# Attention and mixture of experts on one core: score chains of four heads, PV in single tiles, and what reads PSUM in the general path

## The chip, the cores and the metric

One core of one Trainium2 chip runs the whole program. The metric is the device time of one execution in microseconds (us); the median of several executions is given. Engines are PE (TensorE matmuls, PEld its weight loads), DVE (VectorE), ACT (ScalarE), POOL (GpSimd) and SP (SyncE, which issues most DMAs).

## The reference

```python
scores = scale * np.matmul(q, k.transpose(0, 1, 3, 2))      # B=4, H=8, S=768, D=64
keep = is_sink | in_window                                   # 4 sinks, window 128
scores = np.where(keep, scores, -1000000000.0)
a = np.exp(scores - np.max(scores, axis=-1, keepdims=True))
a = a / (np.sum(a, axis=-1, keepdims=True) + 1e-09)
x = np.matmul(a, v)                                          # -> (3072, 512)
logits = x @ w_gate + modality_bias[modality_id]             # 8 experts
e_idx = np.argmax(logits, axis=1)
for e in range(E):
    h = np.maximum(x[mask] @ w1[e], 0.0)                     # mask = e_idx == e, F = 1024
    out[mask] = gate_w[mask, None] * (h @ w2[e])
h = out @ w_in                                               # 512 -> 2048
return (h * (1.0 / (1.0 + np.exp(-1.702 * h)))) @ w_out
```

## The kernel before

The program has four stages in one launch. `attention` (L41) works on 24 tiles `t` of 128 tokens, six for each of four batches, `i = t % 6`; a tile has 8 heads in 4 pairs `c`, two heads `a` beside one another on the array, and a half-tile `g` is two pairs. A query tile sees its own 128 keys, the 128 before and the four sinks, so a score row has 260 columns, and 128 at `i = 0`. In the order of one tile:

- `qtrans`/`ktrans` (L156, L167) transpose queries and keys on PE into PSUM, `qevac` on ACT and `kevac` on DVE copy them out.
- `scores(t, c)` (L194) multiplies for two heads; `mask` (L202, DVE) adds the mask and takes the row maximum, `expo` (L211, ACT) writes the exponentials and their sums.
- `ptrans(t, c)` (L224, L225) transposes the probabilities of two heads; `pevac` copies them to `pts`, DVE for odd `c` (L242), ACT for even (L244). `pts` is a ring of three tiles.
- `pv` (L282) multiplies the values of a key tile with the probabilities of the two query tiles that see it, 256 columns in one product; at `i = 5` the last key tile has 128 columns more (L284). It accumulates in two PSUM banks `ops` that `zero` (L268, ACT) has filled with zeros.
- `oevac` (L291, ACT) copies a half-tile of the output, `back` transposes it back (L301, with a product for the sinks at L298) into PSUM, DVE divides by the sums (L319). Then follow `norm`, `logits` and `pick`, the choice of the expert.

The order of the work is written as a table: `AT` gives for each kind a time in steps of a quarter-tile after the tile's own start, `OPEN` and `MORE` those of the next stage's first work, and `kinds` says how many quarters a call covers. All calls are sorted by time and emitted; each engine runs its instructions in that order. PSUM has eight banks: `NS_BUFS` = 3 for scores, `NT_BUFS` = 3 that `qtrans`, `ktrans`, `ptrans` and `back` share under one tag `t`, and 2 for `ops`. `fill` (L344) issues products without use to PE, 20 before the first scores.

Ahead of it, L1071 and L1072 load a flag into a register on each engine and branch: `general` (L515) is a slow path for other window sizes. It is skipped here, but its buffers share addresses with those of `attention`. After the branch DVE builds the masks (L494 to L507).

Routing sorts tokens by expert. `pair(u, units)` (L1407) runs an expert's 256 tokens; 8 pairs always run, up to 15 by a count known at run time, 12 here, each under an `If`. `more_alone` (L1522) then runs experts on 128 further tokens, 2 here; inside it `second_alone` (L1486) has an `If` (L1496) for the loads of the next expert's weights. `hint` (L1288) tells an engine's branch ahead of time which way it will go, from a register that `values_load` fills (L1290). Last, a dense stage of six groups of 512 tokens (`up`, L1170, and `down`, L1177) multiplies each operand in high and low parts.

Of the kernel before, what the change touches and what calls it, by code (L numbers as in the profile page):

```python
# [29 lines left out]
AT = dict(sinkevac=13.229, oevac=13.14, qevac=-3.201, kevac=-0.864, scores=-0.497, mask0=0.153, mask1=0.329, expo0=0.53, ptrans=2.608, pevac=3.3,  # L30
          expo1=1.235, pv=6.555, qtrans=-4.329, ktrans=-1.83, back=14.129, sinktrans=12.315, norm=14.975, logits=18.7, then=19.826, pick=23.746,
          guard=7.159, invert=12.135, zero=5.2, sinksplit=8.053)
PVU = 2
# [3 lines left out]
OPEN = dict(split1=2.989, x0=5.244, split0=4.299, x1=5.358, split2=5.494, split3=6.448, first0=6.769, first1=7.711, split4=14.718)  # L37
MORE = 85.058, 0.617, 92.724, 1.445


def attention(tc, cst, late, first, spare, q, k, v, wg, xd, then, pick, at_tile, more, opening):  # L41
# [8 lines left out]
    with ExitStack() as ctx:  # L50
# [33 lines left out]
        NV, NG = 6, 3  # L84
        zs = per.tile([P, 1], F32, name="zs")
        nc.gpsimd.memset(zs, 0.0)


        pts = per.tile([P, NG, 4, 2, 2, P], F32, name="pts")
        ops = [ps_o.tile([P, 2, 2, P], F32, name=f"ops{i}") for i in range(2)]  # L90
# [79 lines left out]
        def kevac(t):  # L170
            nc.vector.tensor_copy(kts[:, :, t % NT, 0:P], tps[("k", t)])
# [10 lines left out]
        def scores(t, c):  # L182
# [30 lines left out]
        def where(t, kk):  # L213

            return kk if t % NG else 1 - kk

        def ptrans(t, c):
            i = t % NT
            ps = ps_t.tile([P, 2, 2, P], F32, name=f"pt{t}_{c}", tag="t")
            k0, k1 = where(t, 0), where(t, 1)  # L220
            for a in range(2):
                h = 2 * c + a
                if i > 0:
                    nc.tensor.transpose(ps[:, k0, a, :], pn[t][:, h, 0:P], ident)  # L224
                    nc.tensor.transpose(ps[:, k1, a, :], pn[t][:, h, KB : KB + P], ident)  # L225
                else:
                    nc.tensor.transpose(ps[:, k1, a, :], pn[t][:, h, 0:P], ident)
            tps[("p", t, c)] = ps

        def pview(t, c, x):  # L230
            if t % NT == 0:
                return x[:, t % NG, c, :, t % 2, :]
            a, b = sorted(((t - 1) % NG, t % NG))
            return x[:, a : b + 1 : b - a, c, :, t % 2, :]

        def psrc(t, c):
            ps = tps[("p", t, c)]
            return ps[:, where(t, 1)] if t % NT == 0 else ps

        def pevac(t, c):  # L240
            if c % 2:
                nc.vector.tensor_copy(pview(t, c, pts), psrc(t, c))  # L242
            else:
                nc.scalar.activation(out=pview(t, c, pts), in_=psrc(t, c), func=AF.Copy)  # L244
# [25 lines left out]
        def pv(t, g=None):  # L270

            i = t % NT
            if i == 0:
                return
            kw = dict(start=False, stop=False, skip_group_check=True)
            for j in [t - 1] + ([t] if i == NT - 1 else []):
                for h in range(H) if g is None else range(4 * g, 4 * g + 4):

                    c, a = divmod(h, 2)
                    o = ops[c // 2][64 * a : 64 * a + 64, c % 2]  # L280
                    if j == t - 1:
                        nc.tensor.matmul(o.rearrange("p i t -> p (i t)"), nat[j]["v"][:, h], pts[:, j % NG, c, a].rearrange("p i t -> p (i t)"), **kw)  # L282
                    else:
                        nc.tensor.matmul(o[:, t % 2, :], nat[j]["v"][:, h], pts[:, j % NG, c, a, t % 2, :], **kw)  # L284
# [3 lines left out]
        def oevac(t, g):  # L288
            if g == 0:
                ohl[t] = late.tile([P, 4, P], F32, name=f"oh{t}", tag="oh", bufs=1)  # L290
            nc.scalar.activation(out=ohl[t][:, 2 * g : 2 * g + 2], in_=ops[g][:, :, t % 2, :], func=AF.Copy)  # L291
# [50 lines left out]
        def fill(n):  # L342
            for _ in range(n):
                nc.tensor.matmul(ops[1].rearrange("p c i t -> p (c i t)")[:, 0:256], cst["nothing"][:, 0:P], cst["nothing"], start=True, stop=True)  # L344
# [3 lines left out]
        def ok(t):  # L348
# [3 lines left out]
        kinds = dict(sinkevac=(4, sinkevac), oevac=(2, oevac), qevac=(4, qevac), kevac=(4, kevac), scores=(1, scores), mask0=(1, lambda t, c: mask(t, 2 * c)),  # L352
                     mask1=(1, lambda t, c: mask(t, 2 * c + 1)), expo0=(1, lambda t, c: expo(t, 2 * c)), expo1=(1, lambda t, c: expo(t, 2 * c + 1)),
                     ptrans=(1, ptrans), pevac=(1, pevac), pv=(PVU, pv), qtrans=(4, qtrans), ktrans=(4, ktrans), back=(2, back), sinktrans=(4, sinktrans), norm=(2, norm), logits=(4, logits), then=(4, lambda t: then(t, lgs.pop(t))), pick=(4, pick), guard=(4, guard), invert=(4, invert), zero=(2, zero), sinksplit=(4, sinksplit))
# [3 lines left out]
        for g in range(2):  # L358
            todo.append((len(F2) + .001, zero, (0, g)))
# [1285 lines left out]
```

## Time and profile before

| | |
|---|---|
| median of 3 runs | 1104.44 us (1102.95 to 1104.8) |
| the profiled execution: its own time | 1102.95 us |
| its span in the trace | 1101.4 us |
| mean granted clock of PE | 0.989 |
| busy: PE, DVE, ACT, POOL | 1068.0, 553.7, 418.2, 241.9 us |

Instructions carry the line of kernel.py that issued them. For an engine, a wait is listed with its releaser, the event that ended it; "issue" is time for which nothing is shown. Weight loads (PEld) are issued just ahead of the matmul they belong to, so their start times show the order and the pace of PE. An f32 matmul of the source appears as two instructions.

### The profile page before, as it was taken

To read this page: it belongs to the slowest core of one execution; us is meant where nothing else is said; L and a number is where in the kernel's file an instruction comes from. 1 tells how busy PE (TensorE), PEld (TensorE's weight loads), DVE (VectorE), ACT (ScalarE), POOL (GpSimd) and SP (SyncE) were. 2 spreads that over 40 slices of the span, in tenths; PEclk is the share of its full clock that TensorE was granted. 3 is DMA by queue.
4 is the path that set the end of the run, shared out by engine and by line. 5 is a ranking of instruction groups with operands and counts; after the bars stand their busy time and mean duration, and the time that the engine had idled before them with its cause. 6 is when DMAs were issued, how large, how long until landed. Compare 5 with 4: busy or idle time off the path is not lost. (4 is left out here: it accounts for less than half of the span.)

```text
span 1101.4 us, 18806 instructions
## 1 busy us (share of the span) xinstructions
PE 1068.0 (97%) x6625; PEld 904.5 (82%) x6625; DVE 553.7 (50%) x1385; ACT 418.2 (38%) x1026; POOL 241.9 (22%) x397
## 2 busy tenths in 40 slices
PE   6999999978999999999989999999999999999996
PEld 4676767668999999999978888888888888888885
DVE  3767767886555665522114665655623424334232
ACT  3887778742223332222222332332323222222221
POOL 2532231253243342211001213222200101001011
PEclk8999999998999999999999999999999999999998
DMA  6555565451445532216561322302203303124011
GB/s 122 127 125 126 112 138 118 103 146 60 136 123 161 181 98 79 79 52 197 172 217 55 115 83 73 113 8 70 77 1 115 91 24 116 32 83 153 1 39 39
DMA packets 172115, 108.91 MB, mean 99 GB/s; under 512 B 118000, under 2 KB 149744, under 8 KB 171984
## 3 DMA queue, kind: packets, MB, share of 16 engines
q1 hardware_dynamic: 167184, 91.62, 30.1%
q0 software_dynamic: 4800, 15.73, 4.3%
q8 instruction: 60, 0.98, 0.4%
q14 instruction: 71, 0.58, 0.2%
HBM read 79.85 MB, written 27.48 MB: 97 GB/s over the span
## 5 line engine op out<-in xcount | busy, mean ns | idle before, releaser
L1170 PE MATMUL pu<-xh,wah 128*128 128x256 f32 (+1 forms) x576 | 185.6, 322 | 0.0
L1170 PE MATMUL pu<-xh,wal 128*128 128x256 f32 (+1 forms) x576 | 184.2, 320 | 0.4 <-DVEq L1279 0.4
L1555 DVE TENSOR_TENSOR raw<-pu,raw 128x512 f32<-128x512 f32 x96 | 66.3, 691 | 235.2 <-ACT raw L1554 232.7
L1170 PE MATMUL pu<-xl,wah 128*128 128x256 f32 (+1 forms) x576 | 184.2, 320 | 0.1
L1554 ACT ACTIVATE raw<-pu 128x512 f32<-128x512 f32 x96 | 57.5, 598 | 291.9 <-PE pu L1170 291.2
L1185 PE MATMUL pa<-h,wah 128*128 128x256 f32 x768 | 155.4, 286 | 0.0
L1185 PEld LDWEIGHTS pa<-h,wah 128*128 128x128 f32 x768 | 128.0, 194 | 0.0
L1170 PEld LDWEIGHTS pu<-xh,wal 128*128 128x128 f32 x576 | 110.4, 192 | 8.2 <-DVEq L1279 0.6
L1170 PEld LDWEIGHTS pu<-xh,wah 128*128 128x128 f32 x576 | 110.5, 192 | 7.8 <-ACTq L1279 0.2
L1170 PEld LDWEIGHTS pu<-xl,wah 128*128 128x128 f32 x576 | 110.3, 192 | 7.8 <-DVE xl L1123 0.3
L1185 PE MATMUL pa<-h,wal 128*128 128x256 f32 x384 | 109.6, 285 | 0.0
L1193 ACT ACTIVATE h<-pu 128x256 fp32r<-128x256 f32 x96 | 36.8, 383 | 184.2 <-PE pu L1170 182.6
L202 DVE CUSTOM_DVE_ANT_0 sc<-s,m 128x260 f32<-128x260 f32 (+1 forms) x192 | 73.0, 399 | 51.9 <-PE s L194 46.9
L1196 DVE SCALAR_TENSOR_TENSOR h<-pu,h 128x256 fp32r<-128x256 f32 x96 | 40.3, 422 | 110.8 <-ACT h L1193 61.7
L211 ACT ACTIVATE pn<-sc,mx 128x260 f32<-128x260 f32 (+1 forms) x192 | 92.0, 482 | 5.4 <-DVE mx L202 4.7
L1122 ACT ACTIVATE h<-raw 128x512 fp32r<-128x512 f32 x96 | 60.7, 633 | 77.7 <-DVE raw L1555 77.7
L1177 PE MATMUL pa<-wah,h 128*128 128x512 f32 x216 | 76.4, 390 | 0.0
L1177 PE MATMUL pa<-wbh,h 128*128 128x512 f32 x216 | 76.3, 389 | 0.0
L1170 PE MATMUL pu<-xh,wbh 128*128 128x512 f32 x192 | 74.8, 390 | 1.2 <-ACT y L1493 1.2
L1170 PE MATMUL pu<-xh,wbl 128*128 128x512 f32 x192 | 74.7, 389 | 0.0
L1170 PE MATMUL pu<-xl,wbh 128*128 128x512 f32 x192 | 74.7, 389 | 0.0
L1185 PEld LDWEIGHTS pa<-h,wal 128*128 128x128 f32 x384 | 74.6, 194 | 0.0
(327 smaller groups left out, 2055.8 us busy)
## 6 DMA issues: line engine op xcount, KB each, us to landing
raw<-in_moe_w_dram SPq DMA_DIRECT2D x64, 256.0 KB
cd<-yb SPq DMA_DIRECT2D x20, 512.0 KB
xd<-xe SPq DMA_DIRECT2D x24, 256.0 KB
raw<-yp SPq DMA_DIRECT2D x12, 512.0 KB
qn<-in_q_dram SPq DMA_DIRECT2D x22, 256.0 KB
kn<-in_k_dram SPq DMA_DIRECT2D x22, 256.0 KB
vn<-in_v_dram SPq DMA_DIRECT2D x22, 256.0 KB
yb<-y SPq DMA_DIRECT2D x10, 512.0 KB
```

The source lines that it names most:

```text
L202: nc.vector.tensor_tensor_reduce(out=sc[:, :n], in0=ps[:, :n], in1=m[:, :n], scale=1.0, scalar=3.0e38, op0=ALU.add, op1=ALU.min, accum_out=mx)
L211: nc.scalar.activation(out=pn[t][:, h, :n], in_=sc[:, :n], func=AF.Exp, scale=-1.0, bias=mx, accum_out=sums[t][:, h : h + 1])
L1122: A.activation(out=hi, in_=x, func=AF.Copy)
L1170: nc.tensor.matmul(ps[:, 0:n], w[a][:, s], cols(x, b, k), start=(k == 0 and i == 0), stop=(k == 3 and i == 2))
L1177: nc.tensor.matmul(acc, h[a][:, s], w[b][:, 512:], start=(f == 0 and j == 0), stop=(f == last and j == 2))
L1185: nc.tensor.matmul(acc[:, i % 2 * 256 : i % 2 * 256 + 256], wa[f][a][:, s], h[b], start=(f == 0 and i % 2 == 0 and j == 0), stop=(f == CH ...
L1193: A.activation(out=hi, in_=ps, func=AF.Relu)
L1196: V.scalar_tensor_tensor(out=lo, in0=ps, scalar=0.0, in1=hi.bitcast(F32), op0=ALU.max, op1=ALU.subtract)
L1554: A.activation(out=s, in_=ps, func=AF.Sigmoid, scale=1.702)
L1555: V.tensor_tensor(out=s, in0=ps, in1=s, op=ALU.mult)
```

## The change

- `scores` takes a half-tile: four heads in one call, with a bank each (`NS_BUFS` 4); `AT`, `OPEN` and `MORE` have new times, those behind `pv` about three steps sooner.
- `pv` works on one query tile at a time, 128 columns a product, own keys and the keys before, with start and stop flags, in one bank `ops`. `zero` and the ring are gone; `pts` is a tile of a pool with two buffers.
- `kevac` of the first tile is on ACT.
- In `general`, ACT alone copies from PSUM, and its pools are on the right side of the memory.
- `hint` is a static hint within an `If` on a count that is already in a register; two rows of `sx` are gone; the counts are loaded at f = 3 instead of 5; the hints stand at f = 5, 3 and 2 instead of 6.
- The `If` in `second_alone` is on a register of SP alone.

```diff
-        def scores(t, c):
+        def scores(t, g):
...
-            for a in range(2):
+            for c, a in ((2 * g, 0), (2 * g, 1), (2 * g + 1, 0), (2 * g + 1, 1)):
...
         def kevac(t):
-            nc.vector.tensor_copy(kts[:, :, t % NT, 0:P], tps[("k", t)])
+            if t == 0:
+                nc.scalar.activation(out=kts[:, :, 0, 0:P], in_=tps[("k", t)], func=AF.Copy)
+            else:
+                nc.vector.tensor_copy(kts[:, :, t % NT, 0:P], tps[("k", t)])
...
-        def zero(t, g):
-            nc.scalar.activation(out=ops[g][:, :, t % 2, :], in_=zs.unsqueeze(2).broadcast_to([P, 2, P]), func=AF.Copy)
...
-            for j in [t - 1] + ([t] if i == NT - 1 else []):
-                for h in range(H) if g is None else range(4 * g, 4 * g + 4):
...
-                    if j == t - 1:
-                        nc.tensor.matmul(o.rearrange("p i t -> p (i t)"), nat[j]["v"][:, h], pts[:, j % NG, c, a].rearrange("p i t -> p (i t)"), **kw)
...
+            for c in (2 * g, 2 * g + 1):
+                for kk in range(i == 0, 2):
+                    for a in range(2):
+                        nc.tensor.matmul(ops[64 * a : 64 * a + 64, c], nat[t - 1 + kk]["v"][:, 2 * c + a], pts[t][:, c, kk, a], start=(kk == 0 or i == 0), stop=(kk == 1), skip_group_check=True)
...
-NS_BUFS = 3
+NS_BUFS = 4
...
-        per = ctx.enter_context(tc.tile_pool(name="ge1", bufs=1))
+        per = ctx.enter_context(tc.tile_pool(name="ge1", bufs=1, side="right"))
...
-                    V.tensor_copy(pr[:, j], pt)
+                    nc.scalar.activation(out=pr[:, j], in_=pt, func=AF.Copy)
...
-    def hint(label, row, i):
-        v = nc.values_load(sx[0:1, row, i : i + 1], engines=ENGINES, min_val=0, max_val=1)
-        tc.mark_branch_hint_location(label, v, engines=ENGINES)
+    def hint(label, n, i):
+        with tc.If(n <= i):
+            tc.mark_branch_hint_location(label, "LikelyTaken", engines=ENGINES)
...
-            if f == 5 and u == NP0 - 1:
+            if f == 3 and u == NP0 - 1:
                 counts()
-            if f == 6 and NP0 - 1 <= u < NP - 1:
-                hint(f"pairs{u + 1}", 7, u + 1)
+            if f == (5 if u == NP0 - 1 else 3) and NP0 - 1 <= u < NP - 1:
+                hint(f"pairs{u + 1}", pairs[0], u + 1)
...
+        alone.append(flag(2, E + 1, (ET.SP,)))
...
-            with tc.If(alone[0] > s + 1):
+            with tc.If(alone[1] > s + 1):
```

On PE, a half-tile in the middle of attention before (tile 9's scores, tile 8's transposed probabilities, tile 6's values):

```order
L194 MATMUL s9_0_0_2313<-kts_1141,qt9_2195 128x260
L194 MATMUL s9_0_1_2315<-kts_1141,qt9_2195 128x260
L224 MATMUL pt8_1_2318<-ident_97,pn8_2223 128x128
L225 MATMUL pt8_1_2318<-ident_97,pn8_2223 128x128
L224 MATMUL pt8_1_2318<-ident_97,pn8_2223 128x128
L225 MATMUL pt8_1_2318<-ident_97,pn8_2223 128x128
L156 MATMUL qp10_2323<-ident_97,qn10_2198 128x128 x4
L298 MATMUL bt5_1_2337<-svb0_1637,stt5_2240 128x288
L301 MATMUL bt5_1_2337<-btw_1124,oh5_2234 128x144 x2
L194 MATMUL s9_1_0_2350<-kts_1141,qt9_2195 128x260
L194 MATMUL s9_1_1_2352<-kts_1141,qt9_2195 128x260
L282 MATMUL ops1_1131<-pts_1129,vn6_1656 64x256 x4
```

The same place in the change, from the second pair of scores on, without the products that follow:

```order
L194 MATMUL s9_1_0_2386<-kts_1149,qt9_2265 128x260
L194 MATMUL s9_1_1_2388<-kts_1149,qt9_2265 128x260
L219 MATMUL pt8_1_2390<-ident_97,pn8_2293 128x128
L220 MATMUL pt8_1_2390<-ident_97,pn8_2293 128x128
L219 MATMUL pt8_1_2390<-ident_97,pn8_2293 128x128
L220 MATMUL pt8_1_2390<-ident_97,pn8_2293 128x128
L153 MATMUL qp10_2395<-ident_97,qn10_2276 128x128 x4
L219 MATMUL pt8_2_2422<-ident_97,pn8_2293 128x128
L220 MATMUL pt8_2_2422<-ident_97,pn8_2293 128x128
L219 MATMUL pt8_2_2422<-ident_97,pn8_2293 128x128
L220 MATMUL pt8_2_2422<-ident_97,pn8_2293 128x128
L278 MATMUL bt6_1_2436<-btw_1136,oh6_2349 128x144 x2
```

The two scores ahead of these (s9_0_0, s9_0_1) now stand directly before them, so four heads' scores, three groups of transposes and the back product follow one another; all four of the latter take a buffer of tag `t`. What comes next, with what each waits for:

```order
L278 MATMUL bt6_1_2436<-btw_1136,oh6_2349 128x144 [waits DVE_49,Activation_49]
L278 MATMUL bt6_1_2436<-btw_1136,oh6_2349 128x144
L261 MATMUL ops_1139<-pts7_2245,vn6_1708 64x128 x2
L261 MATMUL ops_1139<-pts7_2245,vn7_1852 64x128 x2
L261 MATMUL ops_1139<-pts7_2245,vn6_1708 64x128 x2
L261 MATMUL ops_1139<-pts7_2245,vn7_1852 64x128 x2
L194 MATMUL s9_2_0_2455<-kts_1149,qt9_2265 128x260
```

The back product waits for DVE and ACT; PV has eight products of 128 columns where four of 256 were.

Behind the branch around `general`, ACT's first rows before:

```order
L1072 UNCONDITIONAL_BRANCH
L1072 UNCONDITIONAL_BRANCH [waits Activation_49]
L161 ACTIVATE qt0_1147<-qp0_1142 128x512 [waits DMAHW3_49,DMAHW2_49,DMAHW4_49,DMAHW1_49,DMAHW5_49,DMAHW0_49,DMAHW6_49,DVE_49,DMAHW7_49,PE_49,Activation_49]
L211 ACTIVATE pn0_1204,sm0_1205<-sc0_0_1192,mx0_0_1193 128x128 [waits DVE_49,Pool_49]
L161 ACTIVATE qt1_1184<-qp1_1179 128x512 [waits PE_49]
L211 ACTIVATE pn0_1204,sm0_1205<-sc0_1_1195,mx0_1_1196 128x128 [waits DVE_49]
```

and in the change:

```order
L1045 UNCONDITIONAL_BRANCH
L1045 UNCONDITIONAL_BRANCH [waits Activation_49]
L158 ACTIVATE qt0_1155<-qp0_1150 128x512 [waits PE_49,Activation_49]
L169 ACTIVATE kts_1149<-kp0_1156 128x4x128 [waits PE_49]
L211 ACTIVATE pn0_1212,sm0_1213<-sc0_0_1197,mx0_0_1198 128x128 [waits DVE_49]
L211 ACTIVATE pn0_1212,sm0_1213<-sc0_1_1207,mx0_1_1208 128x128 [waits DVE_49]
```

The query copy waited for DVE and all eight DMA counters and now waits for PE; the key copy is new there. PE's first transpose loses its wait for DVE in the same way.

## Rows read from the trace of the kernel before

**Rows 1.** Windows: busy us of each engine (count), PE clock, DMA share, GB/s.
```profile
13.20:16.20 3.00, 3.00 (x16) 2.14 (x15) 0.83 (x3) 0.02 (x1) 1.40 (x8) 0.50 1.16 224
17.00:219.00 202.00, 201.07 (x1510) 136.62 (x1510) 144.78 (x609) 162.29 (x559) 60.90 (x199) 1.00 0.56 120
566.00:1101.40 535.40, 525.34 (x2304) 432.31 (x2304) 239.51 (x384) 148.13 (x248) 74.30 (x74) 0.99 0.22 74
```

**Rows 2.** Timeline of weight loads, 94.7 to 99.3 us: start, us, engine, line, names, count.
```profile
94.82 0.30 PEld L194 LDWEIGHTS s<-kts,qt 64*128 64x128 f32 x4 [0.17 <-DVE rs L311]
95.46 0.14 PEld L224 LDWEIGHTS pt<-ident,pn 128*128 128x128 f32 x1 [0.34 <-issue]
...
95.85 0.47 PEld L156 LDWEIGHTS qp<-ident,qn 128*128 128x128 f32 x4
96.28 0.55 PEld L301 LDWEIGHTS bt<-btw,oh 128*128 128x128 f32 x4
96.98 0.30 PEld L194 LDWEIGHTS s<-kts,qt 64*128 64x128 f32 x4
97.62 0.63 PEld L282 LDWEIGHTS ops<-pts,vn 128*64 128x64 f32 x8 [0.34 <-issue]
98.63 0.14 PEld L224 LDWEIGHTS pt<-ident,pn 128*128 128x128 f32 x1 [0.38 <-DVE mx L202]
...
99.22 0.19 PEld L194 LDWEIGHTS s<-kts,qt 64*128 64x128 f32 x2 [0.17 <-issue]
```

**Rows 3.** The start: events of L1072 by engine, then timelines of PE and DVE.
```profile
L1072 PEldq EVENT_SEMAPHORE  x1: 51/51/51, 7.4 to 7.4; - x1
L1072 DVEq EVENT_SEMAPHORE  x1: 21/21/21, 11.2 to 11.2; - x1
...
11.45 1.09 PE L156 MATMUL qp<-ident,raw 128*128 128x128 f32 x4 [6.00 <-DVEq L1072]
...
13.19 3.84 PE L344 MATMUL ops<-raw 128*128 128x256 bf16 x20
...
11.30 0.23 DVE L497 TENSOR_SCALAR raw<-raw 128x128 f32<-128x128 f32 x1 [4.76 <-DVEq L1072]
...
13.12 0.22 DVE L494 TENSOR_SCALAR m<-raw 128x128 f32<-128x128 f32 x1
...
17.48 0.29 DVE L202 CUSTOM_DVE_ANT_0 sc<-s,m 128x128 f32<-128x128 f32 x1 [3.22 <-PE s L194]
```

**Rows 4.** Waits, 530 to 570 us, and events of L1496 (ns min/median/max).
```profile
PE pa L1491 <- SPq L1496: 1.7, 1, 1.7
...
L1496 PEldq COMPARE_BRANCH  x13: 65/185/2503, 537.0 to 563.7; - x13
```

**Rows 5.** Timelines at the end of attention: last scores, first routing product.
```profile
213.11 0.30 PEld L194 LDWEIGHTS s<-kts,qt 64*128 64x128 f32 x4
...
240.83 0.24 PE L825 MATMUL pt<-pk_oh,c_ones 128*128 128x192 bf16 x1 [3.33 <-DVE pk_oh L672]
```

**Rows 6.** Timeline of DVE in the half-tile of rows 2.
```profile
95.67 0.43 DVE L202 CUSTOM_DVE_ANT_0 sc<-s,m 128x260 f32<-128x260 f32 x1 [0.88 <-PE s L194]
...
96.16 0.69 DVE L242 COPY pts<-pt 128x512 f32<-128x512 f32 x1
```

**Rows 7.** Timelines at a batch's last tile: weight loads, then PE.
```profile
68.17 0.58 PEld L284 LDWEIGHTS ops<-pts,vn 128*64 128x64 f32 x8
...
68.39 0.61 PE L284 MATMUL ops<-pts,vn 128*64 128x128 f32 x8
68.93 0.44 PE L227 MATMUL pt<-ident,pn 128*128 128x128 f32 x2
...
L284 PEld LDWEIGHTS ops<-pts,vn x16: 137/137/137, 68.2 to 73.2; 128*64 128x64 f32 x16
```

**Rows 8.** Groups of instructions, 60 to 180 us: busy us, mean ns of one.
```profile
L319 DVE TENSOR_TENSOR xe<-bt,rs 128x288 f32<-128x288 f32 x28 | 12.7, 453 | 1.3 <-PE bt L301 1.1
...
L171 DVE COPY kts<-kp 128x512 f32<-128x512 f32 x14 | 9.5, 680 | 0.0
```

More of the change, by code (lines that the diff above doesn't have):

```diff
@@ L26 @@
 MASKED = 1.0e9
[L30 to L33, printed above, removed]
+AT = dict(sinkevac=10.229, oevac=10.224, qevac=-2.123, kevac=-1.366, scores=-0.449, mask0=-0.2, mask1=0.21, expo0=0.692, ptrans=2.608, pevac=3.437,
+          expo1=0.867, pv=7.004, qtrans=-4.358, ktrans=-1.915, back=10.991, sinktrans=9.575, norm=11.395, logits=15.779, then=16.626, pick=20.835,
+          guard=5.52, invert=11.081, sinksplit=8.614)
 LATE = 0
-OPEN = dict(split1=2.989, x0=5.244, split0=4.299, x1=5.358, split2=5.494, split3=6.448, first0=6.769, first1=7.711, split4=14.718)
-MORE = 85.058, 0.617, 92.724, 1.445
+OPEN = dict(split1=4.183, x0=5.146, split0=3.966, x1=5.358, split2=5.428, split3=6.826, first0=6.763, first1=6.923, split4=14.582)
+MORE = 84.738, 0.617, 92.724, 1.62
 def attention(tc, cst, late, first, spare, q, k, v, wg, xd, then, pick, at_tile, more, opening):
@@ L83, in attention @@
         m0, m1, m2 = cst["m0"], cst["m1"], cst["m2"]
[L84 to L90, printed above, removed]
+        NV = 6
+        ops = ps_o.tile([P, 4, P], F32, name="ops")
+        pts = {}
         sctx = ctx.enter_context(ExitStack())
@@ L219, in ptrans @@
             ps = ps_t.tile([P, 2, 2, P], F32, name=f"pt{t}_{c}", tag="t")
-            k0, k1 = where(t, 0), where(t, 1)
             for a in range(2):
@@ L223, in ptrans @@
                 if i > 0:
[L224 to L225 removed]
+                    nc.tensor.transpose(ps[:, 0, a, :], pn[t][:, h, 0:P], ident)
+                    nc.tensor.transpose(ps[:, 1, a, :], pn[t][:, h, KB : KB + P], ident)
                 else:
[L227 removed]
+                    nc.tensor.transpose(ps[:, 1, a, :], pn[t][:, h, 0:P], ident)
             tps[("p", t, c)] = ps
[L230 to L238, printed above, removed]
         def pevac(t, c):
+            if c == 0:
+                pts[t] = p2.tile([P, 4, 2, 2, P], F32, name=f"pts{t}", tag="pts")
+            k = slice(1, 2) if t % NT == 0 else slice(0, 2)
+            x, ps = pts[t][:, c, k], tps.pop(("p", t, c))[:, k]
             if c % 2:
[L242 removed]
+                nc.vector.tensor_copy(x, ps)
             else:
[L244 removed]
+                nc.scalar.activation(out=x, in_=ps, func=AF.Copy)
         stt, sts = {}, {}
@@ L343, in fill @@
             for _ in range(n):
-                nc.tensor.matmul(ops[1].rearrange("p c i t -> p (c i t)")[:, 0:256], cst["nothing"][:, 0:P], cst["nothing"], start=True, stop=True)
+                nc.tensor.matmul(ops.rearrange("p c t -> p (c t)")[:, 0:256], cst["nothing"][:, 0:P], cst["nothing"], start=True, stop=True)
         fill(F1)
@@ L362, in attention @@
                 t, c = divmod(n, 4)
-                if nm in ("qtrans", "qevac", "ktrans", "kevac", "zero") and t == 0 or nm.startswith("sink") and t % NT < 2:
+                if nm in ("qtrans", "qevac", "ktrans", "kevac") and t == 0 or nm.startswith("sink") and t % NT < 2:
                     continue
@@ L410, in attention @@
         todo.append((last("scores", "mask0", "mask1"), close, (sctx, "scores")))
-        todo.append((last("pv", "zero", "expo0", "expo1"), close, (tctx, "values")))
+        todo.append((last("pv", "expo0", "expo1"), close, (tctx, "values")))
         for nm, time in OPEN.items():
@@ L555, in general @@
                 V.memset(sc, NEG)
+                al = per.tile([P, S], F32, name=f"g_al{i}", tag="al")
                 for g in range(2):
@@ L952, in steps @@
     def steps():
-        sx = pool.tile([P, 9, NQ], I32, name="sx")
+        sx = pool.tile([P, 7, NQ], I32, name="sx")
         V.memset(sx, 0)
@@ L1516, in one @@
                 trans_alone(s + 1)
-            if f == 6 and s + 1 < E:
-                hint(f"alone{s + 1}", 8, s + 1)
+            if f == 2 and s + 1 < E:
+                hint(f"alone{s + 1}", alone[0], s + 1)
             if s == 0 and f % 2:
```

37 lines of the change are left out of this document (12 added, 25 removed).

## The prediction

> **What bounds the kernel now.** I read the stretches first. In attention, 17 to 219 us, PE is busy 201.07 of 202.00 us at a granted clock of 1.00, and in the dense stage, 566 us to the end, 525.34 of 535.40 [rows 1]. The change touches nothing in the dense stage's loop, so what it can win lies in the first half and in the places where PE stops. The reader should see that attention is PE's own time: a second saved on DVE or ACT there is worth nothing, one saved on PE counts in full.
>
> Next, PE's weight loads one by one, over half of a tile (four heads) in the middle of attention [rows 2]. From 94.82 to the next scores but one at 99.22 is 4.40 us, in seven blocks: scores of two heads .64, transposes of probabilities .39, queries .43, back transposes .70, scores .64, PV 1.01, transposes .59. Not all of that is columns. The queries' four transposes of 128 columns take .43, so .107 a piece. Scores and PV work on half of the array, two beside one another. At that pace a score block needs 4 x 260/128 x .107/2 = .43, the back transposes 4 x 144/128 x .107 = .48, PV 8 x 2 x .107/2 = .86. What is over, .21, .22, .15 and .16, falls where the array goes from one shape (64 rows, 64 columns, full) to another. There are five such changes in a half-tile, some .9 us of 4.40.
>
> The view of idle time by releaser gives the rest: at the start ACT, PE and POOL go past the branch around the general path early, but DVE's semaphore event there is at 11.2 us against 7.4 on PE, and PE's first transposes wait until 11.45, the masks are built from 11.30, and DVE's first score row is read at 17.48 [rows 3]. Near the exits of the experts PE waits 1.7 us for SP's branch; PE's own branches of that line last up to 2503 ns [rows 4]. At the end of attention, PE waits 3.33 us for the last choice of experts [rows 5].
>
> **The change, part by part.**
>
> *Order of PE in attention.* With T for the transposes of two heads' probabilities, a half-tile now is scores of four heads, T, queries or keys, T, back transposes, PV: three changes of shape. Free of waits: scores 2 x .43 + .21 = 1.07; T, queries, T 3 x .43 less .04 = 1.25; back .70; PV 1.01; sum 4.03 against 4.40, so .37 less [rows 2].
>
> A wait takes part of that. The transposes, queries, keys and back transposes share three PSUM buffers. Before, scores or PV stood between their uses; now four stand in a row, and the fourth, the back transposes, needs the buffer of the first, which DVE empties. In the trace DVE starts that copy at 96.16, .70 after the first of its transposes at 95.46, and the copy lasts .69 [rows 2, 6]; I add .1 for the release. So the back transposes start no earlier than 1.07 + .70 + .79 = 2.56 instead of 2.32, and a half-tile is 4.27: .13 less than before. Two masks of DVE stand ahead of the copy; the first starts .85 after its scores and the pair is through after some .85 more (.43 each), at 1.7, just before the transposes are (1.77), so they don't delay it [rows 6]. Of 48 half-tiles 8 belong to tiles without a preceding key block, and I count 40: 40 x .13 = 5.2 us less; without the wait 40 x .37 = 14.8.
>
> *PV in pieces of 128 columns.* Twice as many instructions and weight loads, the same columns. The profile has this form already, at a batch's last tile: eight take from 68.39 to 68.93, .54 with the change of shape, no more than .05 a piece, so the columns set the pace [rows 7]. But their eight weight loads of 137 ns took .58, which is (.58 - .137)/7 = .063 apart, slower than the .0535 at which the products consume them; sixteen in a row could run out of the lead. The bounds are 0 and 16 x (.063 - .0535) = .15 a half-tile, so 0 to 6 us; I take a third, +2, since the row nearest to it shows no loss over eight.
>
> On this the Trainium skill speaks against the change: "TensorE: Matmul & The Clock Gate" (the part on sustained throughput of load and matmul pairs) gives some 81 ns a matmul at 128 columns. By that page a half-tile's PV would be 16 x .081 = 1.30 instead of .86, and the whole some 17.6 us more; the row here shows pieces at .0535, so for eight of them the trace does not agree.
>
> *ACT's zeroing* (two a tile) goes. ACT has slack, so nothing by itself. ACT per half-tile keeps four exponentials, a copy, an output copy and half a query copy, all off the path. DVE loses the first key copy alone.
>
> *Start.* PE, ACT, POOL and the loads of tile 2 no longer wait for DVE and all loads after the branch. PE's transposes can go at 7.5 instead of 11.45 [rows 3]. Then 1.9 us for queries and keys, twenty fills that took 3.8 at half clock, .50 granted [rows 1, 3], and scores at about 13.1 at the latest. DVE's masks, if DVE is as late as now, run from 11.30 for 2 us and leave it free at 13.35; the key copy that stood behind them (.69) is ACT's. So the first score row is read at about 13.5 instead of 17.48: 4 us less. In the general path, counted in the order of both kernels, the instructions that are jumped over fall from 240 to 78 on DVE and rise from 36 to 204 on ACT; if the delay follows their number it moves to ACT, whose query and key copies then start at 11.2 and end by 12.4, which gives the same 4. If it vanishes, and the fills run at full clock, it is up to 6; if something else of tile 0 is late, 1. I take 4.
>
> *Tail.* The steps behind the last scores come about three quarter-tiles sooner in the table, but there DVE, ACT and GpSimd work on splits, and PE waits for the choice on DVE at 240.83 [rows 5]. Full quarter-tiles of 2.1 us would give 6; a new order of the splits could cost 3. I take 1 less, near zero, since DVE, not the table, sets the end there.
>
> *Exits.* The branch for the second expert's loads is SP's alone now, so PE's wait of 1.7 us goes [rows 4]. Each hint exchanges a register load for a branch on every engine; PE's median there is 185 ns, and 14 of them would be 2.6 us if none is hidden, about what the 13 branches that go had cost [rows 4]. Between 3.4 less and 1 more I take 1.7 less.
>
> **Sum.** -5.2 + 2 - 4 - 1 - 1.7 = -9.9. The profiled execution took 1102.95, so 1093.1; the median of the three runs stands 1.5 above it. I forecast 1094.
>
> **Rivals.**
>
> 1. *The wait for the buffer does not bind* (the copy is taken sooner, or PE is late anyway): the body gives 14.8 and pieces of PV cost nothing, so -14.8 - 4 - 1 - 1.7 = -21.5, 1081.5. For it: the margin is .24 us a half-tile, of which a part would be found in PE's own queue. Against: all its terms are rows, and the chain S, T, copy, back, PV has no slack in it.
>
> 2. *Slower: weight loads set the pace of PV.* Place: sixteen loads in a row, 40 times, on PE's path. Price: .64 us for each ns above 53.5. With the other terms at -11.9 the kernel is more than .2% (2.2 us, what a measurement here can tell) slower from 14.1/.64 = 22 ns on, at 75 ns a piece; at 85 it is 1102.95 - 11.9 + 20.2 = 1111. For it: loads already lag at .063 [rows 7]. Against: the eight products there weren't held up. By the 81 ns of the Trainium skill named above this rival would end at 1109.
>
> 3. *Entry and exits bring nothing, or the tail takes it back.* The first tile waits for another thing, hints cost what they save. Body alone: 1102.95 - 3.2 = 1099.7; with the tail 3 later, 1103. For it: at the start, DVE's lateness stays unexplained [rows 3]. Against: PE's first wait names it.
>
> 4. *DVE becomes the bound of the half-tile.* With keys it has four masks of some .5, the copy .69, keys .68 and the back product .45 [rows 6, 8]: 3.8 of 4.27. If the back product of the last half runs ahead of the masks, its .45 delays the copy by up to .4, a half-tile by as much, in every other half: 20 x .4 = 8 us, so about 1101.
>
> **How the numbers follow.** Forecast (1088 to 1098) .51; rival 1 .17; rival 2 .09; rival 3 .12; rival 4 .11. Faster: forecast and rival 1 whole, .08 of rival 3, .06 of rival 4, together .82. Same: .03 and .03, .06. Slower: rival 2's .09, .01 and .02, .12. The range 1081 to 1104 takes in both bounds of the body and rivals 3 and 4, and leaves out rival 2 and the ends.
>
> **What would show it.** Right: PE's weight loads at half-tiles of about 4.3 us, with back transposes idle some .2 us before them, released by DVE's copy of transposed probabilities; sixteen PV pieces in about 1 us with the change of shape; first transposes at about 7.5 and first score row at 13 to 14; no wait of PE for SP's branch near the exits. Wrong: half-tiles near 4.0 (rival 1) or over 4.5, with PV over 1.2 (rival 2) or DVE busy ahead of the copy (rival 4); the first score row still after 16, or PE's routing product later behind the last scores than the 27.7 us of now (240.83 less 213.11, [rows 5]).

## The result and the profile after

The change takes 1092.35 us (median of four runs, 1092.1 to 1092.94) against 1104.62 for the kernel before in the same session; the ratio is 0.9889, 95% interval 0.9872 to 0.9906. The forecast was 1094 in a range of 1081 to 1104, against a median of 1104.44. The profiled execution's span is 1090.9 against 1101.4.

Where the gain in span comes from is read at a few marks that both traces have:

| mark | before | after | earlier by |
|---|---|---|---|
| first score row read by DVE | 17.48 | 16.07 | 1.41 |
| first scores of tile 12 | 112.72 | 108.82 | 3.90 |
| first scores of tile 18 | 164.24 | 158.59 | 5.65 |
| first scores of tile 23 | 207.24 | 201.19 | 6.05 |
| first product of routing | 240.83 | 233.01 | 7.82 |
| first product of the single experts | 533.53 | 525.72 | 7.81 |
| first product of the dense stage | 566.37 | 556.16 | 10.21 |

So 1.4 us are from the start, 4.6 from the body of attention, 1.8 from what lies between tile 23's first scores and routing, and 2.4 from the exits of the single experts; the pairs keep their length (292.70 and 292.71), and the dense stage does within .2.

The body first: weight loads of PE in the change, one half-tile and the start of the next, which answer to [rows 2] (start, us, engine, line, names, count, idle time before and its releaser).

```profile
91.30 0.74 PEld L194 LDWEIGHTS s<-kts,qt 64*128 64x128 f32 x8 [0.17 <-DVE xe L296]
92.38 0.14 PEld L219 LDWEIGHTS pt<-ident,pn 128*128 128x128 f32 x1 [0.34 <-PE s L194]
...
92.76 0.47 PEld L153 LDWEIGHTS qp<-ident,qn 128*128 128x128 f32 x4
93.20 0.14 PEld L219 LDWEIGHTS pt<-ident,pn 128*128 128x128 f32 x1
...
93.53 0.14 PEld L220 LDWEIGHTS pt<-ident,pn 128*128 128x128 f32 x1
93.88 0.54 PEld L278 LDWEIGHTS bt<-btw,oh 128*128 128x128 f32 x4 [0.21 <-ACT pn L211]
94.56 0.85 PEld L261 LDWEIGHTS ops<-pts,vn 128*64 128x64 f32 x16
95.59 0.74 PEld L194 LDWEIGHTS s<-kts,qt 64*128 64x128 f32 x8 [0.17 <-issue]
```

A half-tile is 4.29 us (91.30 to 95.59) where it was 4.40. Scores take 1.08, the row of transposes 1.50 with its wait, the back products .68, PV 1.03. The idle .34 and .17 beside the scores stand in [rows 2] as well; what is new is the .21 ahead of the back products. The releaser that the row names, ACT's exponentials, isn't what they wait for: their operand `oh` is ACT's copy of another line, which has ended by 91.81. DVE's timeline of the same stretch tells it:

```profile
92.15 0.43 DVE L202 CUSTOM_DVE_ANT_0 sc<-s,m 128x260 f32<-128x260 f32 x1 [0.95 <-PE s L194]
...
92.50 0.43 DVE L202 CUSTOM_DVE_ANT_0 sc<-s,m 128x260 f32<-128x260 f32 x1
...
93.07 0.69 DVE L231 COPY pts<-pt 128x512 f32<-128x512 f32 x1
```

The copy of the first transposes begins at 93.07, .69 after them (92.38), ends at 93.76, and the back products start .12 later. The two masks ahead of it end in time (by 92.93).

The start: events of the branch around the general path by engine, then timelines of PE and DVE, which answer to [rows 3].

```profile
L1045 PEldq EVENT_SEMAPHORE  x1: 51/51/51, 7.1 to 7.1; - x1
L1045 DVEq EVENT_SEMAPHORE  x1: 21/21/21, 7.4 to 7.4; - x1
L1045 ACTq EVENT_SEMAPHORE  x1: 17/17/17, 10.5 to 10.5; - x1
...
10.54 1.12 PE L153 MATMUL qp<-ident,raw 128*128 128x128 f32 x4 [5.10 <-ACTq L1045]
...
12.30 3.31 PE L321 MATMUL ops<-raw 128*128 128x256 bf16 x20
15.55 0.71 PE L194 MATMUL s<-kts,qt 64*128 64x128 f32 x8
...
16.07 0.29 DVE L202 CUSTOM_DVE_ANT_0 sc<-s,m 128x128 f32<-128x128 f32 x1 [6.51 <-PE s L194]
```

DVE, late before, is on time now (7.4). ACT, on time before, is late (10.5), and PE's first transposes wait for it. Then PE runs its twenty products without use, and the scores follow them. Of the 1.4 us, .9 come from the earlier transposes (10.54 for 11.45) and .5 from the twenty products, which hold the scores up for 3.25 us (12.30 to 15.55) instead of 3.77. That .5 isn't shown to be the change's, and varies by itself: in the trace of experiment 4, whose start is the same, they hold the scores up for 3.86 (12.33 to 16.19), and the first score row is read at 16.71.

The end of attention and the exits, timeline of PE's weight loads (first two lines) and of PE, which answers to [rows 4, 5]:

```profile
204.94 0.74 PEld L194 LDWEIGHTS s<-kts,qt 64*128 64x128 f32 x8 [0.17 <-issue]
206.02 0.12 PEld L247 LDWEIGHTS stp<-identr,st 128*96 128x96 f32 x1 [0.34 <-POOL la L305]
...
233.01 0.32 PE L802 MATMUL pt<-pk_oh,c_ones 128*128 128x192 bf16 x1 [4.14 <-DVE pk_oh L649]
...
525.72 2.94 PE L1456 MATMUL pu<-xs,raw 128*128 128x128 f32 x24 [0.85 <-DVEq L1357]
...
556.16 0.47 PE L1143 MATMUL pu<-xh,wbh 128*128 128x512 f32 x1 [0.78 <-ACT y L1467]
```

The same places in the kernel before, weight loads behind the last scores, then PE:

```profile
213.75 0.63 PEld L282 LDWEIGHTS ops<-pts,vn 128*64 128x64 f32 x8 [0.34 <-issue]
...
563.12 2.02 PE L1491 MATMUL pa<-ca,raw 128*128 128x128 f32 x16 [1.69 <-SPq L1496]
566.37 0.47 PE L1170 MATMUL pu<-xh,wbh 128*128 128x512 f32 x1 [1.23 <-ACT y L1493]
```

PE's wait for SP's branch near the exit (1.69) is gone, and the one ahead of the dense stage is .78 instead of 1.23: 2.1 of the 2.4 us. At the end of attention PE still waits for DVE's choice, even longer (4.14 against 3.33). From the first loads behind the last scores to routing's first product it is 26.99 (206.02 to 233.01) where it was 27.08, so behind the last scores nearly nothing is gained; the 1.8 comes from scores that are issued sooner within tile 23.

### The profile page after: what moved, and what is told of

It reads as the page before. It is cut to its first block, busy times and chain, and to the rows that moved or that the text cites. A ratio compares the mean times of both kernels' runs of the same rounds, so it can differ in the third digit from the quotient of the medians.

```text
span 1090.9 us, 19248 instructions
## 1 busy us (share of the span) xinstructions
PE 1058.8 (97%) x6945; PEld 920.0 (84%) x6945; DVE 551.7 (51%) x1382; ACT 406.9 (37%) x979; POOL 241.3 (22%) x396
## 4 chain that ended last, share of the span: by engine, by line
PE 47%; issue 4%; POOL 0%; ACT 0%; POOLq 0%; DVE 0%; ACTq 0%
PE pu L1143 22%; PE pa L1150 17%; PE pu L1150 6%; PE pu L1456 1%; PE pa L1465 1%; POOL out_dram L1553 0%; POOLq L1615 0%; DVE raw L1529 0%; PE pt L1107 0%; ACT xs L1126 0%; ACT raw L1528 0%; ACT y L1467 0%; ACT ca L1458 0%; POOLq L1553 0%; ACTq L1467 0%
```

## The experiments

Each is an edit of the change, but for the first, which is the kernel before with a part of the change. The first two take the change apart, 3 to 5 ask what the order in attention is worth, 6 to 11 the start and the exits, and 12 repeats the change.

**1. Entry and exits alone.** The kernel before with the general path, the first key copy, the hints and the If of the change.

Three of its places, the others are those of the change:

```diff
+            if t == 0:
+                nc.scalar.activation(out=kts[:, :, 0, 0:P], in_=tps[("k", t)], func=AF.Copy)
...
-                    V.tensor_copy(pr[:, j], pt)
+                    nc.scalar.activation(out=pr[:, j], in_=pt, func=AF.Copy)
...
-            with tc.If(alone[0] > s + 1):
+            with tc.If(alone[1] > s + 1):
```

> The kernel before with only the parts at the entry and the exits of the change: the general path's copies on ACT, the first key copy on ACT, the hints, the If on SP. Attention's order, scores and PV are those of before. By the marks of the two traces the entry gave 1.4 us (first score row read at 16.07 instead of 17.48) and the exits 2.4 (dense stage 10.2 earlier after routing 7.8 earlier). Theory (order of attention is worth most): 1104.6 - 3.8 = 1100.8, with the routing product at about 239.4. Rival (the parts at the entry change addresses and fetches through the whole program, and the order of attention alone is worth little): under 1097.

Measured: 1098.59 against 1103.93 (ratio 0.9952, 0.9935 to 0.9968), so 5.3 less where 3.8 was expected; routing's first product is at 239.14, 1.7 earlier, and the dense stage at 562.00, 4.4 earlier. ACT is late here as well (9.7), and the first score row is read at 15.11. The exits take 30.43 (531.57 to 562.00), as in the change, so these parts alone give the whole 2.4 there. The theory's marks hold within .6, and the rival's 1097 is not reached.

**2. Attention alone.** The change with the general path, hints and If of before.

Two of its places:

```diff
-                    nc.scalar.activation(out=pr[:, j], in_=pt, func=AF.Copy)
+                    V.tensor_copy(pr[:, j], pt)
...
-            with tc.If(alone[1] > s + 1):
+            with tc.If(alone[0] > s + 1):
```

> The change with the general path, the hints and the If as before: chains of four heads, PV in single tiles and the first key copy on ACT alone. Theory (terms add): half-tiles of 4.30 us as in the change, the routing product at 240.8 - 6.4 = 234.4, and a time of 1104.6 - 6.4 = 1098.2. Rival (what the order wins is lost again, since DVE gates the start and the exits meet the old branches later or sooner): over 1101 or under 1096.

Measured: 1095.78 (0.9923, 0.9907 to 0.994), 8.2 less than before, 2.4 better than expected; routing's first product at 234.74, 6.1 earlier. Here DVE is late again (11.1), and the first score row is read at 17.89. The mark at routing is the theory's (234.4) within .4, but the time lies in the rival's range, under 1096: as the rival says, the exits differ although their code is that of before, 31.75 (528.04 to 559.79) for 32.84. The two parts, 5.3 and 8.2, add to 13.5 where the whole gave 12.3 and 11.0 in two sessions; by the spans of the traces it is 4.5 and 6.7 against 10.5. So they are about additive, with attention the larger; the first key copy on ACT is in both parts.

**3. A chain of two.** Scores of two heads a call again; all else as in the change.

```diff
-        def scores(t, g):
+        def scores(t, c):
...
-            for c, a in ((2 * g, 0), (2 * g, 1), (2 * g + 1, 0), (2 * g + 1, 1)):
+            for a in range(2):
...
-scores=(2, scores)
+scores=(1, scores)
```

> The change with scores of two heads a call, as before; PV in single tiles and all times of the table as in the change. A half-tile is then scores, T, queries, scores, T, back products, PV: five changes of shape instead of three, but the second scores stand inside the row of transposes, so the back products find their buffer free. Theory (two changes of shape of .16 to .21 against the wait of .21 to .24): .64 + .39 + .59 + .64 + .43 + .70 + 1.01 = 4.40 a half-tile against 4.30, 40 x .1 = 4 us more than the change, 1096.4, and no idle time ahead of the back products. Rival (the chain of four is worth nothing, the gain came from PV and the missing zeroing): 4.30, 1092.4.

Measured: 1100.08 (0.9963, 0.9949 to 0.9977), 7 to 8 more than the change, where 4 were expected. The weight loads, from one half-tile's scores to the next:

```profile
93.60 0.30 PEld L194 LDWEIGHTS s<-kts,qt 64*128 64x128 f32 x4 [0.17 <-issue]
94.24 0.14 PEld L219 LDWEIGHTS pt<-ident,pn 128*128 128x128 f32 x1 [0.34 <-issue]
94.63 0.47 PEld L153 LDWEIGHTS qp<-ident,qn 128*128 128x128 f32 x4
95.26 0.30 PEld L194 LDWEIGHTS s<-kts,qt 64*128 64x128 f32 x4 [0.17 <-DVE mx L202]
95.90 0.14 PEld L219 LDWEIGHTS pt<-ident,pn 128*128 128x128 f32 x1 [0.34 <-DVE pts L231]
96.29 0.55 PEld L278 LDWEIGHTS bt<-btw,oh 128*128 128x128 f32 x4
96.98 0.85 PEld L261 LDWEIGHTS ops<-pts,vn 128*64 128x64 f32 x16
98.00 0.30 PEld L194 LDWEIGHTS s<-kts,qt 64*128 64x128 f32 x4 [0.17 <-issue]
```

93.60 to 98.00 is 4.40, as worked out, each block within .04, and the back products wait for nothing. So PV in single tiles by itself, with twice the weight loads, leaves the half-tile of before, and the chain of four is what shortens it. The whole costs more than 40 x .1: counted from each kernel's first score row, this one is 3.8 later at tile 12's scores (96.58 against 92.75) and 8.3 later at routing's first product (225.19 against 216.94). A half-tile with a sink product is 4.61 against the change's 4.43 (98.00 to 102.61, and 95.59 to 100.02 in the change): there the difference is .18, not .1. Against the kernel before, too, tile 23's scores come 1.9 later behind the first score row (191.64 for 189.75), so without the chain of four PV in single tiles gains nothing.

**4. PV ahead of the back products.**

```diff
-back=10.991
+back=11.12
```

> The change with the back products ordered behind PV instead of ahead of it. The wait for the third buffer (.21 us before the back products in the trace of the change) is then covered by PV, but there is one more change of shape in a half-tile, at .16 to .22. Theory (buffer wait of .24 against a change of shape of .16): half-tiles of 4.20 instead of 4.30, 40 x .1 = 4 us less than the change, 1088.4. Rival (they are equal, or the later back products delay what follows them): 1092 to 1094, and more behind the last scores.

Measured: 1093.1 (0.9901, 0.9885 to 0.9918), no different from the change. The rival holds in its time:

```profile
91.81 0.74 PEld L194 LDWEIGHTS s<-kts,qt 64*128 64x128 f32 x8
...
94.34 0.85 PEld L261 LDWEIGHTS ops<-pts,vn 128*64 128x64 f32 x16 [0.17 <-ACT pn L211]
95.37 0.54 PEld L278 LDWEIGHTS bt<-btw,oh 128*128 128x128 f32 x4 [0.17 <-DVE mx L202]
96.06 0.74 PEld L194 LDWEIGHTS s<-kts,qt 64*128 64x128 f32 x8
```

The half-tile is 4.25 here, .04 shorter, not .1: an additional change of shape costs nearly what the wait for the buffer costs. Tile 12's scores come 92.65 after the first score row, against 92.75 in the change. What the rival said of the end of attention doesn't hold: routing's first product follows tile 23's first scores by 31.11, in the change by 31.82; but the single experts then start .6 later behind that product (293.30 for 292.71).

**5. Three banks for scores, four for transposes.**

```diff
-NS_BUFS = 4
-NT_BUFS = 3
+NS_BUFS = 3
+NT_BUFS = 4
```

> The change with three PSUM banks for scores and four for transposes, instead of four and three. Theory: the wait for the transposes' buffer goes, but the fourth head's scores need the bank of the first, which DVE's mask leaves some 1.3 us after the scores' start, instead of following at .3 a head: about .6 more in the scores for .24 less at the back products, 4.65 a half-tile, 1092.4 + 40 x .36 = 1107. Rival (DVE empties the first bank early enough): 4.1, 1084.

Measured, one run: 1126.64. The direction is the theory's, the size larger:

```profile
94.65 0.73 PEld L194 LDWEIGHTS s<-kts,qt 64*128 64x128 f32 x6 [0.17 <-DVE mx L202]
95.99 0.29 PEld L194 LDWEIGHTS s<-kts,qt 64*128 64x128 f32 x2 [0.61 <-DVE mx L202]
96.62 0.14 PEld L219 LDWEIGHTS pt<-ident,pn 128*128 128x128 f32 x1 [0.34 <-issue]
...
97.89 0.55 PEld L278 LDWEIGHTS bt<-btw,oh 128*128 128x128 f32 x4
98.58 0.85 PEld L261 LDWEIGHTS ops<-pts,vn 128*64 128x64 f32 x16
99.60 0.73 PEld L194 LDWEIGHTS s<-kts,qt 64*128 64x128 f32 x6 [0.17 <-issue]
```

The back products no longer wait, but the scores last 1.97 instead of 1.08, since the third and the fourth head no longer run side by side on the array: the fourth waits for DVE's first mask (the row's releaser). A half-tile is 4.95. So the fourth score bank is worth some .66 a half-tile, and it is there since PV in single tiles needs one bank instead of two: 4 + 3 + 1 are the eight.

**6. A shorter general path.** ACT copies three or four transposed blocks at a time.

The transposes of the probabilities; those of queries, keys and `x` are changed in the same way:

```diff
-                    pt = ps.tile([P, P], F32, name=f"g_pp{i}{j}", tag="t")
-                    nc.tensor.transpose(pt, sc[:, j * P : j * P + P], ident)
-                    nc.scalar.activation(out=pr[:, j], in_=pt, func=AF.Copy)
+                    pt = ps.tile([P, 3 * P], F32, name=f"g_pp{i}{j}", tag="t")
+                    for n in range(3):
+                        nc.tensor.transpose(pt[:, n * P : n * P + P], sc[:, (j + n) * P : (j + n) * P + P], ident)
+                    nc.scalar.activation(out=pr[:, j : j + 3], in_=pt.rearrange("p (n t) -> p n t", n=3), func=AF.Copy)
```

> The change with the general path written shorter: ACT copies three or four transposed blocks out of one bank at a time, so ACT has 100 instructions in the branch that is jumped over instead of 204, PE 175 rows instead of 229, DVE 78 as in the change. Theory (an engine comes late out of that jump when many of its own instructions are jumped over: DVE with 240 was late, with 78 not; ACT with 36 was not, with 204 was): ACT's semaphore event of the branch at about 7.2 instead of 10.5, PE's first transposes at about 7.4 instead of 10.54, the first score row at 12.8 to 13.2, and 3 us less than the change, 1089.3. Rival (ACT is late because it comes first in PE's wait, or because of the place of its code): event still at 10 to 11, time as the change, 1092.4.

Measured: 1095.81 (0.9925, 0.9909 to 0.9942), and ACT's event is still at 10.5. The theory as put falls: half the number did not help. The rival's event holds, not its time. In the traces the span is 4.5 over the change's (1095.4 against 1090.9): 1.0 by routing's first product (234.01 against 233.01), the rest behind it: the single experts start 294.17 after that product (292.71 in the change), and the dense stage 32.35 after them (30.44). Of the latter, PE waits .97 for the branch that the change has on SP alone:

```profile
558.61 1.13 PE L1467 MATMUL pa<-ca,raw 128*128 128x128 f32 x8 [0.97 <-SPq L1472]
```

**7. Shorter still.** All outputs of a head and all logits are copied at once as well, so ACT's first row behind the jump is its row 82.

Beside the edits of 6:

```diff
-                nc.scalar.activation(out=xo[:, i], in_=po, func=AF.Copy)
+            nc.scalar.activation(out=xo, in_=pos, func=AF.Copy)
...
-            nc.scalar.activation(out=cst["wide"][:, t], in_=pl, func=AF.Copy)
+        nc.scalar.activation(out=cst["wide"][:, 0:T], in_=pl, func=AF.Copy)
```

> The change with the general path shorter still: three or four transposed blocks, all six outputs of a head and all logits are copied by ACT at once, so ACT's first instruction behind the jump is its row 82 instead of 214 (110 in the run before this, where ACT stayed late at 10.5). Theory (an engine is late when what it jumps to lies more than some hundred instructions ahead on its own list: DVE late at row 257, not at 96; ACT not late at 46, late at 110 and 214): ACT's event at about 7.2, PE's first transposes at 7.3, first score row at about 12.8, 3.2 us less at the start than the change. What the exits cost may move by 1 to 3 us, since all code behind moves: 1089 to 1092. Rival (ACT is late whatever the length, once it reads PSUM in that path): event at 10 to 11, first score row near 16, 1092 to 1096.

Measured: 1091.35 (0.9887, 0.987 to 0.9903). Event of the branch on ACT, then timelines of PE and DVE:

```profile
L1047 ACTq EVENT_SEMAPHORE  x1: 17/17/17, 7.1 to 7.1; - x1
...
7.45 1.09 PE L153 MATMUL qp<-ident,raw 128*128 128x128 f32 x4 [2.01 <-PEq L1047]
...
12.46 0.71 PE L194 MATMUL s<-kts,qt 64*128 64x128 f32 x8
...
12.98 0.29 DVE L202 CUSTOM_DVE_ANT_0 sc<-s,m 128x128 f32<-128x128 f32 x1 [3.31 <-PE s L194]
```

ACT is on time and the first score row 3.1 earlier than in the change, as expected. At tile 12 all of it is there (105.74 against 108.82), at routing 2.7; of the whole, 1.0 is left. The single experts start 293.39 behind routing (.7 more), and the dense stage 31.65 behind them (1.2 more).

**8. Eight products without use.**

```diff
-F1 = 20
+F1 = 8
```

> The change with 8 products without use ahead of the first scores instead of 20. Theory (the first scores wait for these products alone, since ACT's copies of queries and keys end at 13.15 and the sinks' keys at 13.47, while the 20 products end at 15.5): first scores at 13.6 to 14.3 instead of 15.55, 1.5 us less, 1090.9. Rival (PE runs at half speed for longer without them, or the loads of the second tile come too late): first score row earlier, but the scores of tile 12 at 108.8 as now, 1092.4.

Measured: 1091.7 (0.989, 0.9874 to 0.9907). First scores at 13.87, tile 12 at 107.14, both 1.7 earlier than in the change, and 1.45 at the dense stage (554.71). ACT's event is at 10.5 in both traces, so the start can be compared, and there the theory holds; the medians, .65 apart, can't tell it from no difference.

**9. The If on all engines.**

```diff
-            with tc.If(alone[1] > s + 1):
+            with tc.If(alone[0] > s + 1):
```

> The change with the If for the second expert's loads back on all engines; hints as in the change. Theory (the wait near the exit came from that If): dense stage 32.1 to 32.8 us behind the start of the single experts instead of 30.4, 1.7 to 2.4 us more, 1094.5. Rival (it came from the register loads of the hints): 30.4, 1092.4.

Measured: 1092.43 (0.9903, 0.9887 to 0.992), and the dense stage 30.65 behind the single experts (524.37 to 555.02). The theory falls: with the new hints and the If on all engines the exit is .2 longer, not 1.7 to 2.4.

**10. The old hints.**

The register load; the old places in the loop and the two rows of `sx` are back as well:

```diff
-        with tc.If(n <= i):
-            tc.mark_branch_hint_location(label, "LikelyTaken", engines=ENGINES)
+        v = nc.values_load(sx[0:1, row, i : i + 1], engines=ENGINES, min_val=0, max_val=1)
+        tc.mark_branch_hint_location(label, v, engines=ENGINES)
```

> The change with the old hints (a register load each, in the old places, and their two rows of the table) and the If on SP alone. Theory (the If was the cost): dense stage 30.4 us behind the start of the single experts, routing to single experts 292.7 as before and after, 1092.4. Rival (the hints were the cost): 31.5 to 32.8 us, 1094.

Measured: 1093.72 (0.9913, 0.9897 to 0.993), dense stage 31.37 behind the single experts. That is .9 more than in the change and just short of the rival's 31.5. By these two traces the hints matter more than the If; but experiments 6 and 7, which touch neither, move the same stretch by 1.9 and 1.2, so the .9 and the .2 can't be put down to these edits for certain. Timeline of PE at the first product of the dense stage with the old hints, and with the If on all engines:

```profile
555.97 0.47 PE L1147 MATMUL pu<-xh,wbh 128*128 128x512 f32 x1 [1.43 <-ACT y L1471]
```

```profile
555.02 0.47 PE L1143 MATMUL pu<-xh,wbh 128*128 128x512 f32 x1 [0.79 <-issue]
```

**11. Shorter path and eight products.** Edits 7 and 8 together; what it has beside 7:

```diff
-F1 = 20
+F1 = 8
```

> The shorter general path and 8 products without use together. Theory (both shorten the same start): first score row at 11.2 instead of 12.98 or 14.39, scores of tile 12 at 104.0, and 1091.35 - 1.6 = 1089.7, since the exits cost what they cost with the shorter path. Rival (loads of the second and third tile, or DVE's masks, now set the start): tile 12 at 105.0 or later, 1091.

Measured: 1090.61 (0.9877, 0.9861 to 0.9894), the fastest here, though its interval meets the change's. The rival holds at the start. PE, and the stretch 12.6 to 15.6 by windows (busy us of each engine, then PE's granted clock, DMA share and GB/s) in this experiment, in 7 and in the change:

```profile
9.18 0.71 PE L194 MATMUL s<-kts,qt 64*128 64x128 f32 x8
11.71 0.66 PE L153 MATMUL qp<-ident,raw 128*128 128x128 f32 x4 [1.82 <-DMA raw<-in_q_dram]
...
12.60:15.60 3.00, 3.00 (x18) 2.29 (x19) 0.51 (x4) 1.28 (x5) 0.00 (x0) 0.50 1.10 241
12.60:15.60 3.00, 3.00 (x30) 2.46 (x31) 1.53 (x12) 2.28 (x10) 0.00 (x0) 1.00 1.18 254
12.60:15.60 3.00, 3.00 (x22) 2.20 (x20) 0.00 (x0) 0.55 (x1) 1.40 (x8) 1.00 0.90 194
```

The first scores come at 9.18, and the first score row at 9.70, 1.5 sooner than the theory had it: PE's first eight transposes begin at 7.31 and take .90, where in experiment 7 they took 1.74 (7.45 to 9.19), both at a granted clock of 1.00, for a reason that no run shows. But then PE waits 1.82 for the second tile's queries, and after that idle time the granted clock is .50 (the 1.2 of its two levels, 1.2 and 2.4 GHz) for some three us. Tile 12's scores come at 105.75, as with experiment 7 (105.74). What is gained over 7 is at the exits: 30.43 instead of 31.65.

**12. The change again.**

> The change itself once more, to see how much the marks of one execution move with nothing changed. Theory (where code lies decides how late an engine comes out of a jump): ACT's event again at 10.5, first score row at 16.0 to 16.2, routing product within .3 of 233.0, dense stage within .3 of 556.2. Rival (it is chance): ACT's event anywhere from 9.0 to 10.5, as in the other runs, and marks that move by 1 us.

Measured: 1093.09 (0.99, 0.9884 to 0.9917). Routing at 232.98 and the dense stage at 555.94: within .3 as the theory says, but ACT's event is at 10.1 and the first score row at 15.75, where it had 10.5 and 16.0 or later. Of the rival, the moving event holds, marks that move by 1 us don't. ACT's event is 2.7 behind PE's here and 3.4 in the first trace, so the delay itself moves by .7 with nothing changed, and the marks at routing and behind it hardly follow.

## Why the prediction was right, and where not

- **The shape changes and the buffer wait** were right in mechanism and size. A half-tile was to be 4.27 with PV's loads free; it is 4.29. Back products were to start 2.56 after the scores, released by DVE's copy; they start at 2.58. The .1 for the release, for which the prediction has no row, is .12 in the trace. Rival 1 (no wait, half-tiles near 4.0) falls with this, and rival 4 with DVE's masks, which end before the copy begins. Experiment 3 brings back five changes of shape and with them 4.40; 4 and 5 show both ways of removing the wait, and that neither pays.
- **PV in pieces of 128 columns**: the +2 us did not come. Sixteen pieces take 1.03 with the change of shape (94.56 to 95.59), against 1.01 for eight of twice the width, and their loads last .85 in all, so .05 apart: they keep pace. Of the bounds 0 and 6 the lower was true. Rival 2 falls with this. The Trainium skill's 81 ns at 128 columns ("TensorE: Matmul & The Clock Gate", Back-to-back issue gap) would, by estimate, be 1.30 for the sixteen; the trace, with 1.03, doesn't agree for these pieces, which work side by side on half of the array.
- **Body**: -5.2 + 2 = -3.2 was forecast; -4.6 is measured up to tile 23 (6.05 less 1.41). Without the wrong +2 the term is .6 from the measured one.
- **Start**: -4 was forecast, -1.4 came, and the first score row at 16.07 is the prediction's own sign of being wrong ("still after 16"). Here rival 3 held, a first tile that waits for another thing, though not at the exits. The prediction named the case that happened, the delay moving from DVE to ACT, but gave it the same 4 us. The step that failed is "PE's transposes can go at 7.5": in the order PE's first transpose waits for ACT too (below), so transposes, fills and scores stand behind ACT's event (10.5) as they stood behind DVE's (11.2). With ACT on time (experiment 7) the first score row is at 12.98, 4.5 sooner than before. Ahead of the prediction the order was read for ACT's rows and for the wait on DVE that PE loses, not for the one that it keeps. A slip beside it is small: the 1.9 us for queries and keys are 1.74 in its rows (11.45 to 13.19).

```order
L153 MATMUL qp0_1150<-ident_97,raw0_69 128x128 [waits DMAHW2_49,PE_49,Activation_49]
```

- **Tail**: -1 forecast, -1.8 measured from tile 23's first scores on (7.82 less 6.05). Behind the last scores it is only .1 (27.08 to 26.99), and the wait for DVE's choice grew from 3.33 to 4.14. Near zero, since DVE sets the end there, was right for what follows the last scores; the rest comes from the last tile's own order.
- **Exits**: -1.7 forecast, -2.4 measured. The wait that was named went, 1.69 of the 2.4, and .45 more ahead of the dense stage. That the `If` on SP alone took it away isn't shown: with the `If` back on all engines (9) the stretch is .2 longer and with the old hints (10) .9, and in neither does PE wait for SP's branch; with both back (2) it waits .27; and in experiment 6, which touches neither, .97. With both as before the stretch is 31.75 (2), in the kernel before 32.84 with the same code of that stage. What makes PE wait for SP's branch in one program and not in another stays open. The bound of 3.4 less has no working in the prediction.

So the time was nearly right, .15% from the forecast, partly by luck, because errors met: the start gave 2.6 less than forecast, and body, tail and exits together 2.9 more.

## What to carry to other kernels

Where an engine is busy without a gap, look at its start times one by one: what the columns don't explain is the price of the order, here .15 to .22 for each change of the array's shape, and grouping like work pays that back until the wait for a buffer that isn't empty yet takes its place. When a wait is moved from one engine to another, read in the order every engine that the first instruction behind it waits for; if the new one is among them, nothing has been won yet. And where a saving early in a program of many branches is small, follow it by marks: 3.1 us at the start were 1.0 at the end.

## What the runs showed of the hardware

- DVE and ACT, where they jumped over much of their own code, came out of the jump 2 to 4 us late. Rows counted in the order of the program: DVE at its row 257 (11.2) but not at 96 (7.4); ACT not at 46 (7.2) nor 82 (7.1), but at 110 (10.5) and 214 (10.5). PE was on time at row 267 (7.4). The Trainium skill says in "Runtime: NRT & Kernel Launch" (Instruction fetch mechanics) that a taken branch to a target that isn't yet held must wait for a fetch. DVE's and ACT's events agree with that, though no run shows the fetch itself; PE's doesn't show it. The same section of the Trainium skill gives PE four times the instruction memory of most engines. The delay behind PE's event was 3.4, 2.7, 2.0 and 2.0 in four traces in which ACT's rows up to the jump are the same (the change, the change again, experiments 9 and 10), and lay between these in experiment 3 (2.5).
- Shortening code that never runs (experiments 6 and 7) moved stretches hundreds of us later by .7 to 1.9 us. That the place of the code behind does this isn't shown: the shorter path with fewer fills (11) had the exits of the change again (30.43), and the cause stays open.
- The granted clock was .50 after PE had waited 1.82 us at the start of experiment 11, and 1.00 in the same stretch of experiment 7, in which PE hadn't waited. The wait alone doesn't settle it: in the change PE had waited 5.10 us ahead of 10.54, and the clock in that stretch was 1.00; in experiment 4, with the same start, 5.12 us ahead of 10.57, and it was .51. Nor does the granted clock alone give the pace of PE there: the twenty products without use held the scores up for 3.25 us in the change and for 4.25 in experiment 2 (13.12 to 17.37), both at 1.00.
